# Hash attention followed by a SwiGLU block: VectorE's order at the ends of groups, and both rows of a pair in sequence

## The chip, the core and the metric

The kernel runs on one core of a Trainium2 chip. Its time is the device time of one execution in microseconds; the comparison uses the median of several runs. A core has a matrix engine (TensorE: PE in the profile, with the weight loads on a row of their own, PEld), a vector engine (VectorE: DVE), a scalar engine (ScalarE: ACT), a general engine (GpSimd: POOL) and a queue engine (SyncE: SP). Each works through its own list of instructions, and they wait for each other through semaphores.

## The reference

Two blocks follow each other. The first is attention in which a query sees only the keys with the same hash:

```python
# q, k, v: (4, 8, 768, 64), proj: (64, 6), all float32
q_bits = (np.einsum('bhsd,dk->bhsk', q, proj) > 0)      # six sign bits for each row
k_bits = (np.einsum('bhsd,dk->bhsk', k, proj) > 0)
mask = q_bucket[:, :, :, None] == k_bucket[:, :, None, :]
scores = np.where(mask, scale * np.matmul(q, k.transpose(0, 1, 3, 2)), -1e9)
attn = np.exp(scores - max); attn = attn / (attn.sum(-1) + 1e-09)
x = np.matmul(attn, v)                                   # then (B, H, S, D) -> (B*S, H*D) = (3072, 512)
```

The second is a gated feed-forward block on the 3072 rows that come out:

```python
g = x @ w_gate                       # 512 -> 1536
silu = g * (1.0 / (1.0 + np.exp(-g)))
out = (silu * (x @ w_val)) @ w_out   # 1536 -> 512
```

## The kernel before

There are four batches `b`, and in each of them four pairs of heads, so sixteen pairs `n`. A pair has two rows (`half`): 384 queries against all 768 keys, in six steps `c` of 128 keys. One row is a stage of TensorE: 36 matmuls for the scores (tile `sc`) and 24 for the product with `v` (tile `av`). ScalarE takes the exponentials, VectorE adds up the six tiles of them (`acc`). After both rows of a pair, `total` sums `acc` over the keys on TensorE (tile `sum`), takes the reciprocal on VectorE and spreads it by DMA; `norm` later multiplies it in. After a batch's last pair its feed-forward work is put on the list `atoms`.

```python
    def add(u):                     # after each step c of a row, on VectorE
        if c == 1:
            acc[n, half] = att.tile([P, 2, HQ], FP32, tag="acc", name="acc")
            nc.vector.scalar_tensor_tensor(out=acc[n, half], ...)              # L523
        elif c > 1:
            nc.vector.tensor_tensor(acc[n, half], acc[n, half], a[:, :, 0:HQ], op=ALU.add)  # L527
    def total(n):
        ps = ... bank("sum")
        for h in range(2):
            for half in range(2):
                nc.tensor.matmul(ps[g : g + BLOCK, 0:HQ], ones, t[half][:, h, :], ...)   # L540
        nc.vector.reciprocal(r, ps[:, 0:HQ])                                   # L548
        ...                                                  # eight DMAs spread r over t
        waiting.append(lambda: norm(n, t))                                     # L560, VectorE
        if pr == NP - 1:
            push_ffn(b)
```

The feed-forward work of a batch is nine groups: six up groups (both up projections and the gate) and three down groups (one chunk of 128 columns for each of the two rows). Both are written as Strassen products: fewer matmuls on TensorE, paid for with additions on VectorE. In batches 1 to 3 an up group has ten steps (68 matmul records in the profile). Two of its seven products are split once more (`deeper`), and the weights of these inner products are formed on VectorE by `weigh`, four additions of 128x128 (`r3`, `r2`, `r1`, `r4`). A function `look_ahead` calls `weigh(0)` of the group that stands first on `atoms`, if it has not been called yet.

```python
    def look_ahead():
        if atoms:
            finish(getattr(atoms[0][1], "ahead", []))

            def weigh(d):
                for o, p, q, op in ((r3, v11, v21, ALU.subtract), (r2, v22, r3, ALU.subtract),
                                    (r1, r2, v11, ALU.add), (r4, v12, r2, ALU.subtract)):
                    plus(o, p, q, op)
            ...
            def step(at):
                if at == 0:
                    while first:           # the batch's additions on x: 16 of them, once a batch
                        first.pop(0)()
                    finish(ahead)          # weigh(0), if it is not done yet
                for do in todo[at]:
                    do(at)
                if at == len(todo) - 1:
                    look_ahead()
                    settle(at + NB)        # what is left of the gates of this group
            # steps 0, 1: two outer products; step 2 begins with inner products on v11, r1, v12
```

The down part needs sums of the hidden values. `combine(i, 1)` forms `s1`, `combine(i, 2)` `s2`, `combine(i, 3)` `s3` in place, `combine(i, 4)` `s4`; each is done in two halves over the hidden blocks, `part` 0 and 1. Part 0 of the first chunk is `early`, which is tied to the last step of the last up group:

```python
    def down_strassen(out_of):
        def chunk(i):
            def step(n):
                if n == 0 and i == 0:
                    while next(preparing, None):
                        pass
                    for which in (1, 2, 3):
                        combine(0, which, 1)
                a, w, to = ((a11, b11, "a"), (s1, t1, "b"), (s2, t2, "a"), (a12, b21, "c"),
                            (s3, t3, "a"), (s4, b22, "b"), (a22, t4, "a"))[n]
                product(c, [(a[:, f], w[:, f]) for f in range(NFP)], ...)     # 12 matmul records
                ...
                for part in range(2):
                    if n == 0:
                        combine(i, 4, part)
                    elif n in (3, 4) and i + 1 < CH:
                        for which in ((1,), (2, 3))[n - 3]:
                            combine(i + 1, which, part)
        ...
        return lambda: [combine(0, which, 0) for which in (1, 2, 3)]

    def push_ffn(b):
        up_strassen(x, b, first)
        at = len(atoms) - 1
        early = down_strassen(out_of)
        size, last, end = atoms[at]
        atoms[at] = (size, lambda: (early(), last()), end)
```

The main loop goes over the 32 rows. From pair 4 on, every row is followed by a stretch of groups from `atoms` (a "gated stretch"). Groups are taken whole, as long as a credit is above zero: 14 units a row at first, and 15.75 from pair 8 (the third batch of pairs) on; a group is 14 units. In between stand the next pair's preparations (`chores`): two transposes on VectorE (`turn_q`, `turn_k`) and the hashes (TensorE tile `hps`, then ScalarE, a DMA and VectorE). What is left of `atoms` after the last row is done in one go, which is called the tail below.

```python
    for u in range(0, N, NCH):
        n, half, _ = units[u]
        gating = u >= LATE                                   # from pair 4 on
        ...
        for c in range(NCH):
            score(u + c)                                     # PE sc, ACT exp
            if c:
                add(u + c)
        if n >= 2 * NP:
            look_ahead()
        if ... or (n >= 2 * NP and half == 0):
            finish(waiting)                                  # norm of the pair before
        for c in range(NCH):
            attend(u + c)                                    # PE av
        if half == 1:
            load(n + 2, "qkv" if n + 2 > NP else "v")
        finish(first)                                        # the batch's 16 additions on x
        if half == 1 and n >= NP:
            total(n)
            if n + 1 < len(pairs):
                chores = [None] + steps.pop(0)()             # hashes: before the groups
        if not gating:
            continue
        if n + 1 < len(pairs) and half == 0:
            steps = front(n + 1)
            chores = [None, steps.pop(0), None, steps.pop(0)]   # both transposes
        credit += 14 if n < 2 * NP else 15.75
        while atoms and (credit > 0 or not end):
            size, atom, end = atoms.pop(0)
            credit -= size
            atom()
            ...                                              # chores, one for each unit
    for _, atom, _ in atoms:                                 # the tail
        atom()
```

Of the kernel before, what the change touches and what calls it, by code (L numbers as in the profile page):

```python
# [18 lines left out]
def kernel(  # L19
# [13 lines left out]
    B, H, S, D = q.shape  # L33
# [3 lines left out]
    CH = NCH // 2  # L37
    HQ = CH * P
    BLOCK = 32
    NP = H // 2  # L40
# [28 lines left out]
    def bank(name):  # L69
        return banks.tile([P, 512], FP32, tag="ps", name=name)  # L70


    pairs = [(b, pr) for b in range(B) for pr in range(NP)]
# [34 lines left out]
    def load(n, names):  # L108
        if n < len(pairs):
            for name in names:  # L110
                fetch(n, name, nc.sync)
# [83 lines left out]
    NB = 7  # L195
# [67 lines left out]
    def as_words(t):  # L263
        return t.bitcast(I32).rearrange("p (f w) -> p f w", w=2)

    spots = [hid[:, half, m].rearrange("p f q -> p (f q)") for half in range(2) for m in range(2)]
    early = [as_words(t[:, 0 : 2 * PIECE]) for t in spots]
# [33 lines left out]
    def scale_ahead():  # L301
        scale_to(min(progress["piece"] + 4, progress["scaled"] + 1))
# [70 lines left out]
    def prepare_on(n):  # L373
        for _ in range(n):
            next(preparing, None)
# [9 lines left out]
    atoms = []  # L385
# [195 lines left out]
    def finish(todo):  # L581
        while todo:
            todo.pop(0)()
# [6 lines that stand above are left out]
    def product(ps, pairs_, start):  # L590

        for i, (a, x) in enumerate(pairs_):
            nc.tensor.matmul(ps, a, x, start=start and i == 0, stop=i == len(pairs_) - 1,  # L593
                             skip_group_check=True)

    def plus(o, a, b, op=ALU.add):
        nc.vector.tensor_tensor(o, a, b, op=op)  # L597
# [162 lines left out]
        for i in range(NG // 2):  # L760
            both(i)

    def down_strassen(out_of):


        t2, t3, t4 = down_t
        t1 = b12
        s2, s1, s4 = down_s

        def parts(i, fs):  # L770
            return [hid[:, half, m, fs, i * P : (i + 1) * P]
                    for half in range(2) for m in range(2)]

        def combine(i, which, part):
            fs = slice(part * NFP // 2, (part + 1) * NFP // 2)
            a11, a12, a21, a22 = parts(i, fs)
            if which == 1:
                plus(s1[:, fs], a21, a22)
            elif which == 2:
                plus(s2[:, fs], s1[:, fs], a11, ALU.subtract)  # L780
            elif which == 3:
                plus(a21, a11, a21, ALU.subtract)
            else:
                plus(s4[:, fs], a12, s2[:, fs], ALU.subtract)

        def chunk(i):
            now = {}

            def step(n):
                a11, a12, s3, a22 = parts(i, slice(None))  # L790
                if n == 0 and i == 0:
                    while next(preparing, None):
# [4 lines that stand above are left out]
                    for name in "cba":  # L797
                        now[name] = bank("po")[:, 0:HD]
                    o = word_room[0]
                    now["o"] = [[o[:, (2 * r + x) * HD : (2 * r + x + 1) * HD] for x in range(2)]  # L800
                                for r in range(2)]
                a, w, to = ((a11, b11, "a"), (s1, t1, "b"), (s2, t2, "a"), (a12, b21, "c"),
                            (s3, t3, "a"), (s4, b22, "b"), (a22, t4, "a"))[n]
                c = now[to]
                product(c, [(a[:, f], w[:, f]) for f in range(NFP)], n in (0, 1, 3))
                r, x = ((0, 0), (1, 1), (0, 1), (0, 0), (1, 1), (0, 1), (1, 0))[n]
                o = now["o"][r][x]
                if n in (3, 4, 5):
                    plus(o, o, c)
                else:  # L810
                    nc.scalar.copy(o, c)  # L811
                if n >= 3:
                    nc.sync.dma_start(out_of(r, i)[:, x * HD : (x + 1) * HD], o)
                for part in range(2):
                    if n == 0:
                        combine(i, 4, part)
                    elif n in (3, 4) and i + 1 < CH:
                        for which in ((1,), (2, 3))[n - 3]:
                            combine(i + 1, which, part)

            for n in range(NB):
                atoms.append((2, lambda n=n: step(n), n == NB - 1))

        for i in range(CH):
            chunk(i)
        return lambda: [combine(0, which, 0) for which in (1, 2, 3)]

    def push_ffn(b):
        x = [xT[b, pr] for pr in range(NP)]
        rows = out[b * S : (b + 1) * S, :].rearrange("(p c) m -> p c m", c=NCH)  # L830

        def out_of(half, i):
            return rows[:, half * CH + i, :]

        up_strassen(x, b, first)
        at = len(atoms) - 1
        early = down_strassen(out_of)
        size, last, end = atoms[at]
        atoms[at] = (size, lambda: (early(), last()), end)

# [6 lines left out]
    def prepare_pair(count):  # L849
        for _ in range(count):  # L850
            rest.extend(f for f in steps.pop(0)() or [] if f)
# [4 lines left out]
    credit = 0.0  # L856
    for u in range(0, N, NCH):
        n, half, _ = units[u]
        gating = u >= LATE
        if u == MOVE:  # L860
            progress["late"] = True
            for t in late_ring:
                nc.gpsimd.memset(t[:, :, HQ:AW], 1.0)
        for c in range(NCH):
            score(u + c)
            if u + c == 2 or not gating and half == 1 and c == 2:
                prepare_pair(1)
            if c == 1 and half == 0 and 0 < n <= NP:
                total(n - 1)
            if c:  # L870
                add(u + c)
        if n >= 2 * NP:
            look_ahead()
        if (n < NP and half == 1) or u == LATE or (n >= 2 * NP and half == 0):
            finish(waiting)
        finish(rest)
        if not gating and half == 0:
            steps = front(n + 1)
        if not gating and half == 0 and u > 0:
            prepare_pair(2)  # L880
        for _ in range(1 if u else 2):
            scale_ahead()
        for c in range(NCH):
            attend(u + c)
        if not gating:
            scale_ahead()
        if half == 1:
            load(n + 2, "qkv" if n + 2 > NP else "v")
        elif not gating:
            prepare_pair(2 if u > 0 else 4)  # L890
            if n + 2 <= NP:
                load(n + 2, "qk")
        finish(first)
        prepare_on(0 if u == LATE else 4)
        chores = []
        if half == 1 and n >= NP:
            total(n)
            if n + 1 < len(pairs):
                chores = [None] + steps.pop(0)()
        prepare_on(0 if LATE - NCH <= u <= LATE else 3 if gating or not half else 1)  # L900
        if not gating:
            continue
        if n + 1 < len(pairs) and half == 0:
            steps = front(n + 1)
            chores = [None, steps.pop(0), None, steps.pop(0)]

        credit += 14 if n < 2 * NP else 15.75
        end = True
        part = 0
        while atoms and (credit > 0 or not end):  # L910
# [3 lines that stand above are left out]
            part += size  # L914
            if n < 2 * NP and part >= 11 or u + NCH == N and part >= 6:
                finish(waiting)
                if u + NCH == N:
                    finish([first.pop(0) for _ in range(min(2, len(first)))])
            if 5 < part < 14 if u == LATE else part < (9 if u < LATE + 3 * NCH else 11):
                prepare_on(size)  # L920
            if 6 < part < 11 or u == LATE and part > 10:
                scale_ahead()
            for _ in range(size):
                if chores:
                    step = chores.pop(0)
                    chores.extend(step and step() or [])
        while chores:
            step = chores.pop(0)
            chores.extend(step and step() or [])
    for _, atom, _ in atoms:  # L930
        atom()


# [30 lines left out]
```

The softmax here doesn't subtract the row's maximum and nothing guards it: scores larger than these inputs give would overflow.

## Time and profile before

| what | value |
|---|---|
| time, median of 3 runs | 995.05 us (994.68 to 995.08) |
| span of the profiled execution | 992.9 us |
| PE busy | 980.0 us, 99% |
| DVE busy | 670.4 us, 68% |
| ACT busy | 408.1 us, 41% |
| POOL busy | 127.3 us, 13% |
| granted clock of TensorE | 0.999 |
| HBM traffic over the span | 100 GB/s |

In the profile a busy share says how long an engine had an instruction of its own under way. Ends of matmuls are modelled, so for TensorE it is safer to read where the next matmul starts. The chain of waits follows the work that ended last back through the program: a piece on PE means that TensorE was the one everybody waited for then, a piece on DVE or ACT in the middle of PE pieces means that TensorE stood still until that instruction was done. All additions through the helper `plus` carry line L597, all Strassen matmuls L593; they are told apart by tile: `up` and `po` are the PSUM tiles of the up and down groups, `inner` holds the formed inner weights of `weigh(0)`, `room` (128x384) the down sums `s1`, `s2` and `s4`.

### The profile page before, as it was taken

To read this page: it belongs to the slowest core of one execution; us is meant where nothing else is said; L and a number is where in the kernel's file an instruction comes from. 1 tells how busy PE (TensorE), PEld (TensorE's weight loads), DVE (VectorE), ACT (ScalarE), POOL (GpSimd) and SP (SyncE) were. 2 spreads that over 40 slices of the span, in tenths; PEclk is the share of its full clock that TensorE was granted. 3 is DMA by queue.
4 is the path that set the end of the run, shared out by engine and by line. 5 is a ranking of instruction groups with operands and counts; after the bars stand their busy time and mean duration, and the time that the engine had idled before them with its cause. 6 is when DMAs were issued, how large, how long until landed. Compare 5 with 4: busy or idle time off the path is not lost.

```text
span 992.9 us, 13575 instructions
## 1 busy us (share of the span) xinstructions
PE 980.0 (99%) x4813; PEld 625.0 (63%) x4813; DVE 670.4 (68%) x1276; ACT 408.1 (41%) x921; POOL 127.3 (13%) x248
## 2 busy tenths in 40 slices
PE   9999999999999999999999999999999999999998
PEld 4444555555577766656566775666666786666687
DVE  5899888888965556777784457776776446667631
ACT  7999555566512234444442313443342202323200
POOL 3222232231100011111010001111100001121000
PEclk9999999999999999999999999999999999999999
DMA  8777685875303042433322114343121112233001
GB/s 235 218 249 229 157 259 178 228 269 157 106 26 76 16 121 79 104 92 84 99 81 57 52 31 108 98 107 100 57 87 33 35 34 85 75 117 105 1 30 35
DMA packets 119987, 107.02 MB, mean 108 GB/s; under 512 B 90032, under 2 KB 104848, under 8 KB 119920
## 3 DMA queue, kind: packets, MB, share of 16 engines
q0 software_dynamic: 18336, 73.29, 23.0%
q1 hardware_dynamic: 100784, 32.67, 14.2%
q8 instruction: 38, 0.62, 0.3%
q10 hardware_dynamic: 800, 0.20, 0.1%
q14 instruction: 29, 0.24, 0.1%
HBM read 81.79 MB, written 17.30 MB: 100 GB/s over the span
## 4 chain that ended last, share of the span: by engine, by line
PE 91%; DVE 5%; issue 2%; ACT 2%; POOL 0%; DMA 0%; DVEq 0%; ACTq 0%; POOLq 0%
PE up L593 41%; PE po L593 21%; PE sc L494 14%; PE av L509 11%; PE sum L540 1%; PE hps L412 1%; DVE c L571 1%; DVE hid L575 1%; PE tps L396 1%; DVE hid L597 1%; DVE room L368 0%; DVE inner L597 0%; PE idle L134 0%; DVE acc L527 0%; ACT th L570 0%
## 5 line engine op out<-in xcount | busy, mean ns | idle before, releaser
L593 PE MATMUL up<-xT,room 128*128 128x384 f32 (+1 forms) x732 | 243.0, 465 | 0.0
L593 PEld LDWEIGHTS up<-xT,room 128*128 128x128 f32 x732 | 134.8, 190 | 73.3 <-issue 9.8
L593 PE MATMUL up<-xc,room 128*128 128x384 f32 (+1 forms) x540 | 176.9, 455 | 0.0
L327 POOL DMA_DIRECT2D room<-ram x144 | 77.9, 543 | 677.8 <-PE up L593 662.4
L494 PE MATMUL sc<-qT,kT 64*128 64x384 f32 x768 | 161.0, 494 | 0.0
L597 DVE TENSOR_TENSOR c<-c,up 128x192 f32<-128x192 f32 (+1 forms) x198 | 78.9, 406 | 80.9 <-PE up L593 76.5
L527 DVE TENSOR_TENSOR acc<-acc,A 128x768 f32<-128x768 f32 x128 | 122.7, 958 | 15.7 <-ACT A L497 2.9
L593 PEld LDWEIGHTS up<-xc,room 128*128 128x128 f32 x540 | 99.2, 190 | 43.8 <-DVE c L597 1.1
L570 ACT ACTIVATE th<-c 128x384 f32<-128x384 f32 x90 | 46.9, 522 | 158.1 <-DVE c L571 89.7
L497 ACT ACTIVATE A<-sc 128x384 f32<-128x384 f32 x256 | 103.9, 528 | 0.6 <-PE sc L494 0.5
L494 PEld LDWEIGHTS sc<-qT,kT 64*128 64x128 f32 x768 | 67.9, 186 | 54.3 <-issue 40.5
L811 ACT COPY words<-po 128x256 f32<-128x256 f32 x48 | 17.9, 373 | 199.0 <-PE po L593 180.1
L597 DVE TENSOR_TENSOR hid<-hid,up 128x192 f32<-128x192 f32 (+1 forms) x162 | 67.5, 418 | 43.5 <-PE up L593 41.6
L509 PE MATMUL av<-A,vraw 128*64 128x384 f32 (+1 forms) x512 | 88.2, 486 | 0.0
L597 DVE TENSOR_TENSOR words<-words,po 128x256 f32<-128x256 f32 x36 | 15.2, 421 | 99.2 <-PE po L593 99.2
L679 ACT COPY c<-up 128x384 f32<-128x384 f32 x72 | 34.4, 478 | 88.8 <-PE up L593 88.7
L593 PE MATMUL po<-wo,room 128*128 128x256 f32 x288 | 66.6, 380 | 1.5 <-DVE room L597 1.5
L593 PE MATMUL po<-wo,hid 128*128 128x256 f32 x288 | 66.9, 382 | 0.0
L593 PE MATMUL po<-room,hid 128*128 128x256 f32 x288 | 66.1, 379 | 0.0
L509 PEld LDWEIGHTS av<-A,vraw 128*64 128x64 f32 x512 | 36.7, 137 | 46.1 <-issue 44.1
L494 PE MATMUL sc<-qb,kb 64*128 64x384 bf16 x384 | 65.1, 323 | 0.5 <-DVE kb L426 0.5
L593 PEld LDWEIGHTS po<-wo,hid 128*128 128x128 f32 x288 | 54.1, 190 | 12.1 <-issue 4.9
(137 smaller groups left out, 1165.3 us busy)
## 6 DMA issues: line engine op xcount, KB each, us to landing
room<-ram POOLq DMA_DIRECT2D x96, 384.0 KB, 3.7
vraw<-in_v_dram SPq DMA_DIRECT2D x16, 384.0 KB, 3.3
ram<-room POOLq DMA_DIRECT2D x12, 512.0 KB, 5.1
room<-ram POOLq DMA_DIRECT2D x48, 128.0 KB, 3.5
out_dram<-words SPq DMA_DIRECT2D x48, 128.0 KB, 1.7
room<-in_moe_w_out_dram POOLq DMA_DIRECT2D x10, 512.0 KB, 6.4
qraw<-in_q_dram SPq DMA_DIRECT2D x48, 96.0 KB, 3.2
hid<-in_moe_w_gate_dram POOLq DMA_DIRECT2D x9, 512.0 KB, 6.8
```

Of the source, the lines that this page charges most:

```text
L327: nc.gpsimd.dma_start(places[k % 2][:, PARTS[go], :], ram[k % NG][:, PARTS[go], :])
L396: nc.tensor.transpose(ps[:, i * P : (i + 1) * P], raws[name, n][:, half * CH + i, :, :].rearrange("p h d -> p (h d)"), ident)
L412: nc.tensor.matmul(tile_[i * BLOCK : (i + 1) * BLOCK, 0:HQ], hash_w, T[name, n][:, half * HQ : (half + 1) * HQ], start=True, stop=True)
L494: nc.tensor.matmul(sc[h], x["k", n][rows, ks], x["q", n][rows, qs], start=start, stop=not start)
L497: nc.scalar.activation(weights(u)[:, h, 0:HQ], sc[h], AF.Exp, scale=SCALE * (OFF / 2 if n <= NP else 1.0))
L509: nc.tensor.matmul(ps[h * D : (h + 1) * D, 0:width], raws["v", n][:, h, c, :], a[:, h, 0:width], start=c == 0, stop=c == NCH - 1)
L527: nc.vector.tensor_tensor(acc[n, half], acc[n, half], a[:, :, 0:HQ], op=ALU.add)
L570: nc.scalar.activation(th, g, AF.Tanh, scale=0.5)
L593: nc.tensor.matmul(ps, a, x, start=start and i == 0, stop=i == len(pairs_) - 1, skip_group_check=True)
L597: nc.vector.tensor_tensor(o, a, b, op=op)
L679: nc.scalar.copy(tile_of(g, spot), c)
L811: nc.scalar.copy(o, c)
```

## The change

Three places put VectorE's instructions at the end of a group in another order, and one changes the large order of work.

1. The tail now takes each group off the list before it runs it, so that `look_ahead` at the end of a group finds the next group there instead of the first one of the tail.
2. In the last batch the first down chunk takes its fourth product (on `a12`) as the second one, so that `s1` is needed one product later.
3. In all batches but the last, `early` comes after the last step of the last up group rather than before it.
4. From pair 8 on (`whole`), both rows of a pair follow each other, and one gated stretch with the credit of both (31.5) follows. The next pair's transposes and loads come in its first group, the hashes after its first 14 units; the norm of the pair before and the batch's additions on x stay behind the first row.

```diff
-    def down_strassen(out_of):
+    def down_strassen(out_of, at_once):
...
-            def step(n):
+            order = (0, 3, 1, 2, 4, 5, 6) if at_once and i == 0 else range(NB)
+
+            def step(at):
+                n = order[at]
...
-                    elif n in (3, 4) and i + 1 < CH:
-                        for which in ((1,), (2, 3))[n - 3]:
+                    elif at in (3, 4) and i + 1 < CH:
+                        for which in ((1,), (2, 3))[at - 3]:
...
-        early = down_strassen(out_of)
+        early = down_strassen(out_of, b == B - 1)
         size, last, end = atoms[at]
-        atoms[at] = (size, lambda: (early(), last()), end)
+        atoms[at] = (size, lambda: (early(), last()) if b == B - 1 else (last(), early()), end)
...
+        whole = n >= 2 * NP
...
-        if n >= 2 * NP:
+        if whole and half:
             look_ahead()
...
-        if half == 1:
+        if whole:
+            pass
+        elif half == 1:
             load(n + 2, "qkv" if n + 2 > NP else "v")
...
-            if n + 1 < len(pairs):
+            if n + 1 < len(pairs) and not whole:
                 chores = [None] + steps.pop(0)()
...
-        if not gating:
+        if not gating or whole and not half:
             continue
-        if n + 1 < len(pairs) and half == 0:
+        if n + 1 < len(pairs) and whole:
+            turn_q, turn_k, hashes = front(n + 1)
+            chores = 5 * [None] + [turn_q, None, turn_k, lambda: load(n + 2, "qkv")]
+            chores += 5 * [None] + [hashes]
+        elif n + 1 < len(pairs) and half == 0:
             steps = front(n + 1)
             chores = [None, steps.pop(0), None, steps.pop(0)]
-        credit += 14 if n < 2 * NP else 15.75
+        credit += 31.5 if whole else 14
...
-    for _, atom, _ in atoms:
-        atom()
+    while atoms:
+        atoms.pop(0)[1]()
```

## The prediction

> **What bounds the kernel now.** I read the page first (busy shares, granted clock), then the waits of TensorE alone, then the chain of waits in order of time, and last the timelines of PE and DVE at the joints which these point to.
>
> ```profile
> PE 980.0 (99%) x4813; PEld 625.0 (63%) x4813; DVE 670.4 (68%) x1276; ACT 408.1 (41%) x921; POOL 127.3 (13%) x248
> PEclk9999999999999999999999999999999999999999
> ```
>
> TensorE has matmuls under way for 99% of the span, at full clock. A change that removes no matmul can therefore win only where TensorE stands still, or where matmuls follow each other more slowly than their kind needs. The waits of TensorE (total us, times, longest):
>
> ```profile
> PE up L593 <- DVE inner L597: 5.7, 5, 1.1
> PE po L593 <- DVE room L597: 1.5, 2, 1.0
> ```
>
> Five waits for the inner weights and two for the down sums: 7.2 us that this view admits. The chain of waits (start, length, what) shows where. In the tail:
>
> ```profile
> 822.10 17.50 PE up L593 x68
> ...
> 839.62 0.56 DVE hid L597
> 840.17 0.48 DVE c L571
> ...
> 840.68 0.53 ACT th L570
> ...
> 841.23 0.56 DVE c L571
> ...
> 842.18 0.55 DVE hid L575
> 842.73 0.21 DVE inner L597
> ...
> 843.29 0.30 DVE inner L597
> ...
> 843.63 14.86 PE up L593 x58
> ...
> 862.53 14.86 PE up L593 x58
> ```
>
> A group that nothing disturbs takes 17.50 us (68 records). In the tail, groups begin their inner products 862.53 - 843.63 = 18.90 us apart. The loss is 1.40 us a joint, and its cause stands between: `weigh` (inner) comes after the whole chain of gates of the group before. The same chain earlier, at the row after a batch's last up group, and at the first row of the third batch of pairs:
>
> ```profile
> 323.74 5.05 PE sc L494 x36
> 328.79 4.04 PE av L509 x24
> 332.83 18.33 PE po L593 x84
> ...
> 507.17 3.47 PE sc L494 x21
> 510.68 2.30 PE sc L494 x13
> 512.99 4.04 PE av L509 x24
> ```
>
> Scores take 5.05 us elsewhere, but 512.99 - 507.17 = 5.82 us here (and 5.81 us at 747.61): 0.77 us lost each time. The timeline of DVE there has the three `early` additions from 506.50 to 508.03, in front of the group's last additions. Those free the PSUM banks which the scores need. The two `po` waits are 654 + 104 ns late at 280.4 (start to start, against the usual 216 ns) and 1155 + 104 ns late at 938.95.
>
> **What the Trainium skill says.** "TensorE: Matmul & The Clock Gate", section Architectural detail, calls VectorE and ScalarE strict FIFOs, while TensorE may only pull weight loads ahead. The trace agrees: `inner` at 842.73 does nothing that needs the gates, and still waits behind a gate which waits for a ScalarE instruction (840.68 to 841.21). So the order in the program decides. "Perfetto Trace Analysis", section Optimization Strategy, advises to find the gaps on the busiest engine and what blocks them, and to make those dependencies start sooner; that is what changes 1 to 3 do. "TensorEngine Tiling (Array Packing)", section Key Properties, states that changing the tiling mode drains TensorE; that would be the reason for change 4. The trace shows a price: the last `up` record before a row's scores is followed 93 ns later than usual, and the second score record another 201 ns later; from `av` to `up` it is 100 and then 104 ns.
>
> **The change part by part.**
>
> *1. Tail.* Six up groups, five joints. After it `weigh` stands behind the group's last plus and two gate instructions, before the gate that waits for ScalarE. That order already runs in the gated stretches of the kernel before: there the group's last plus starts at 452.11 and `r1` ends at 454.45, 2.34 us later. At the tail's joint the last plus starts at 839.62, so `r1` would be ready at 841.96. TensorE's first product on `inner` would follow the record of 842.16 by 163 ns, at 842.32. There are 0.36 us to spare, the wait goes wholly: 5 x 1.40 = 7.0 us.
>
> *2. First down chunk of the last batch.* `s1` part 1 is ready at 938.90. With `a12` second, the product on `s1` begins two products of 12 x 0.216 = 2.59 us after 933.91, at 939.09, and its second half later still. `a12`'s last block is written by the gates that end at 938.3, and its last two records start at 933.91 + 22 x 0.216 = 938.66: that fits. Gain 1.155 + 0.104 = 1.26 us.
>
> *3. `early` behind the last step.* At 507 and 748 the banks come free 1.5 us earlier, the scores run through: 2 x 0.77 = 1.5 us. In batch 0 only the order changes. The 0.76 us at 280.4 comes from a VectorE that is full from 257 to 281, and stays.
>
> *4. Rows in sequence.* For each of eight pairs one exit `av` to `up` (204 ns) and one entry `up` to `sc` (294 ns) become one `av` to `sc`, which costs 101 + 201 = 302 ns in the first pairs (75.14 us): 0.196 x 8 = 1.6 us. Against it, the hashes of seven pairs now stand between groups instead of beside the sum. Sum and hashes together took 1.59 us from the first `sum` record to the first `up` record (377.63 to 379.22), the sum alone 0.77 us (784.80 to 785.57), so the hashes cost 0.82 us there. Between two `up` records I take 0.78 + 0.09 + 0.10 = 0.97 us, and up to 0.33 us more than before where the sum is the short kind: 7 x 0.15 to 0.33, about -1.3 us. What is left of part 4 itself: +0.3 us.
>
> The new cost lies in VectorE behind the first row. In the third and the fourth batch of pairs, at its first pair (8 and 12), 16 additions on x stand between the two rows. In the kernel before a gated stretch followed them, now the second row's `acc` additions do, and `sum` waits for those:
>
> ```profile
> 327.62 4.14 DVE L527 TENSOR_TENSOR acc<-acc,A 128x768 f32<-128x768 f32 x4
> 331.68 1.02 DVE L597 TENSOR_TENSOR xc<-xT 128x384 f32<-128x384 f32 x2
> ...
> 338.05 0.36 DVE L597 TENSOR_TENSOR words<-xc,words 128x192 f32<-128x192 f32 x1
> ```
>
> Pair 8: the row starts on TensorE at 323.74. The first row's sums are done at 331.68 (+7.94 us), the additions at 338.32 (+6.64), and five more `acc` instructions take 5.13 us (326.55 to 331.68): 343.45, that is 19.71 us after the start. TensorE has both rows done after 2 x 9.09 = 18.2 us, and waits 1.5 us. Pair 12: the norm of 0.93 us comes in too (572.12 to 573.05), so 20.65 us and a wait of 2.5 us. Sum: -4.0 us. At the other pairs the second row's sums are done 7.9 us after its start, within its 9.1 us.
>
> In all: 7.0 + 1.3 + 1.5 + 0.3 - 4.0 = 6.1 us. 995.05 - 6.1 = 988.95, said as 989.0 us.
>
> **The rivals.**
> *A. All joints are clean, and the additions on x hide.* Then 4.0 us more, 985.0 us. For it: VectorE is busy only 68%. Against it: the sum cannot start before the last `acc`, and VectorE keeps its order.
> *B. The wait moves into the new joints.* From pair 8 on, six joints between up groups lie inside a stretch; if each loses the 1.40 us of the tail, 8.4 us go and the time is 997.4 us. For it: at these joints no row of 9.1 us lies between any more, and the first group carries the reciprocal of 2.56 us and two transposes of 0.9 us. Against it: `look_ahead` works there as in the gated stretches before (454.45), and VectorE is busy 12.46 of 18.90 us in a tail group, with gaps of 1.13 and 0.86 us where the transposes fall.
> *C. The loads collide.* The loads of q, k and v are now issued when the next group's weights are fetched (POOL's `room<-ram`, landing 3.6 us after issue). If they doubled that to 7 us, the weights fetched about 8.5 us before the next group would still be there in time. Little, some 1 to 2 us at worst.
> *D. Change 4 saves far more, because the switch is dearer than it looks.* Against it: nothing but the 0.2 us a pair shows in the starts of matmuls.
>
> **Range and chances.** All of the sure gains together (7.0 + 1.3 + 1.5 + 1.6 us) make 11.4 us or 1.1%, so 2% faster (975.1 us) is out of reach. 2% slower (1014.9 us) would need 26 us of new waits, more than rival B and the sums' waits together. Within the range the sums' waits (3 to 5 us) and the new joints (0 to 3 us) decide; 985.5 to 992.5 us should hold it. Faster by over 2%: 0.01, within: 0.97, slower: 0.02.
>
> **What would show it.** In the changed profile the waits of TensorE for `inner` should be gone, and the chain should show six tail groups 17.5 us apart, without DVE pieces. Scores of 5.05 us should stand where 5.82 us was. Two waits of `sum` for `acc` (L540 for L527), of 1.5 and 2.5 us, should be new, at the first pair of the third and fourth batch of pairs. A wait of `po` for `room` should remain once, near 280 us. I am wrong if `inner` still holds up `up` inside the stretches (B), if no wait for `acc` appears (A), or if the scores of the second row wait.

## The result and the profile after

| | before | after |
|---|---|---|
| time, median | 995.07 us (994.68 to 995.16, 4 runs) | 989.68 us (989.58 to 989.87, 4 runs) |
| span of the profiled execution | 992.9 us | 988.0 us |
| PE busy | 980.0 us | 978.8 us |
| DVE busy | 670.4 us | 669.3 us |

The ratio is 0.9947 with a 95% interval of 0.9930 to 0.9964: 5.4 us or 0.5% faster, where 6.1 us and 989.0 us were predicted. The engines do the same work as before; what changed is how long TensorE stands still. The waits of TensorE in the changed kernel (total us, times, longest):

```profile
PE sum L540 <- DVE acc L527: 2.7, 2, 1.8
...
PE po L593 <- DVE room L597: 0.5, 1, 0.5
PE po L593 <- ACT words L815: 0.5, 1, 0.5
```

The five waits for `inner` are gone and one of the two for `room` as well. Two waits of `sum` for `acc` are new, as predicted, and so is one of `po` for `words`, which was not. The chain of waits of the changed kernel (start, length, what) shows the tail and the last down groups:

```profile
770.26 54.59 PE po L593 x252
824.84 104.89 PE up L593 x408
929.73 10.37 PE po L593 x48
940.11 0.02 issue
940.13 0.38 ACT words L815
940.51 0.04 issue
940.55 44.31 PE po L593 x204
```

Six up groups run as one piece of 104.89 us, which is 17.48 us a group; before, a group and its joint took 18.90 us. From the first `up` record of the tail to the first `po` record it is 104.89 us now and was 111.98 us (821.94 to 933.91), so 7.1 us are won. But four products into the last batch's first down chunk TensorE waits for a ScalarE copy. The sum of pair 8, in the chain of the same kernel:

```profile
326.66 0.97 DVE acc L523
...
331.88 0.94 DVE xc L597 x2
...
338.16 0.36 DVE words L597
338.52 0.88 DVE acc L523
...
342.68 0.97 DVE acc L527
343.65 0.04 issue
343.69 0.85 PE sum L540 x6
344.54 18.33 PE po L593 x84
```

For 17 us this chain runs over VectorE: `acc` of the first row, the additions on x, `acc` of the second row, then the sum. A long piece of VectorE in the chain does not mean that TensorE stands still all that time: it works on both rows meanwhile, starts the sum's first record at 341.93 and only then has to wait. From the first `sum` record to the next `po` record it is 2.54 us here and 3.40 us at pair 12, against 0.78 us at the other pairs: 1.76 + 2.62 = 4.4 us. (The view of waits says 2.7 us, as it counts from the modelled end of two `sum` records that could start early.)

An undisturbed pair of the changed kernel in the same chain:

```profile
398.81 5.05 PE sc L494 x36
...
416.96 0.78 PE sum L540 x8
417.75 18.97 PE up L593 x72
436.72 0.78 PE hps L412 x8
437.50 16.39 PE up L593 x64
453.89 1.32 PE sc L494 x7
```

From scores to scores it takes 453.89 - 398.81 = 55.08 us. The same pair took 55.10 us before (from 396.97 to 452.07). The rows in sequence bring 0.02 us at such a pair.

### The profile page after: what moved, and what is told of

It reads as the page before. It is cut to its first block, busy times and chain, and to the rows that moved or that the text cites. A ratio compares the mean times of both kernels' runs of the same rounds, so it can differ in the third digit from the quotient of the medians.

```text
span 988.0 us, 13667 instructions
## 1 busy us (share of the span) xinstructions
PE 978.8 (99%) x4813; PEld 621.7 (63%) x4813; DVE 669.3 (68%) x1276; ACT 409.7 (41%) x921; POOL 127.2 (13%) x248
## 4 chain that ended last, share of the span: by engine, by line
PE 90%; DVE 6%; ACT 2%; issue 2%; POOL 0%; DMA 0%; DVEq 0%; ACTq 0%; POOLq 0%
PE up L593 42%; PE po L593 22%; PE sc L494 13%; PE av L509 10%; DVE acc L527 2%; PE sum L540 1%; PE hps L412 1%; ACT A L497 1%; DVE xc L597 1%; PE tps L396 1%; DVE room L368 0%; ACT room L497 0%; PE idle L134 0%; DMA room<-ram 0%; DVE acc L523 0%
```

## The experiments

Times are medians. Each was compared with the kernel before on the same chip, which stood at 994.95 to 995.19 us every time. Spans are those of the profiled execution.

### The tail's list alone (change 1 in the kernel before)

```diff
-    for _, atom, _ in atoms:
-        atom()
+    while atoms:
+        atoms.pop(0)[1]()
```

> The kernel before with the tail's list handling alone (change 1). Theory: the five waits for the inner weights go, 5 x 1.40 = 7.0 us, so 988.1 us; the tail's up groups take 105 us instead of 112 us on TensorE, nothing else moves. Rival: the gates that now come later hold up something else in the next group (PSUM banks, the gate tiles), and only part of the 7 us comes; then 990 to 994 us, and a new wait of up appears.

988.26 us (988.07 to 988.91), ratio 0.9931 (0.9917 to 0.9946). No wait for `inner` is left, the waits for `room` are both there as before:

```profile
PE po L593 <- DVE room L597: 1.5, 2, 1.0
```

So two lines bring 6.8 us, more than the whole change does.

### Both rows in sequence alone (changes 1 to 3 undone)

```diff
-            order = (0, 3, 1, 2, 4, 5, 6) if at_once and i == 0 else range(NB)
+            order = range(NB)
...
-        atoms[at] = (size, lambda: (early(), last()) if b == B - 1 else (last(), early()), end)
+        atoms[at] = (size, lambda: (early(), last()), end)
...
-    while atoms:
-        atoms.pop(0)[1]()
+    for _, atom, _ in atoms:
+        atom()
```

> The changed kernel with changes 1 to 3 undone, so both rows in sequence alone. Theory: the two waits of the sum for the last acc cost 1.8 + 2.6 = 4.4 us, and the switches saved around the rows come back around the hashes, so 995.1 + 4.3 = 999.4 us; joints inside the stretches are clean. Rival (switches saved, hashes free): 8 x 0.2 us less, 997.8 us. Rival (joints inside a stretch cost 1.4 us): about 1004 us or more.

999.01 us (998.79 to 999.25), ratio 1.0039 (1.0025 to 1.0053): slower than before by 3.9 us. The waits of TensorE are all of the old ones and the new one:

```profile
PE up L593 <- DVE inner L597: 5.7, 5, 1.1
PE sum L540 <- DVE acc L527: 2.7, 2, 1.8
PE po L593 <- DVE room L597: 1.5, 2, 1.0
```

The five waits for `inner` are those of the tail; none was added at the joints inside the stretches. This rules out the prediction's rival B for this kernel.

### Changes 1 to 3 without the sequence

The kernel before with these parts of the change; the main loop stays as it was.

```diff
+            order = (0, 3, 1, 2, 4, 5, 6) if at_once and i == 0 else range(NB)
...
-        atoms[at] = (size, lambda: (early(), last()), end)
+        atoms[at] = (size, lambda: (early(), last()) if b == B - 1 else (last(), early()), end)
...
-    for _, atom, _ in atoms:
-        atom()
+    while atoms:
+        atoms.pop(0)[1]()
```

> Changes 1 to 3 without the rows in sequence. Theory: 7.1 (tail) + 1.55 (scores after early) + 0.5 (last down chunk, where one wait is replaced by a shorter one) = 9.2 us less than before, 985.9 us, that is faster than the changed kernel by 3.8 us. Rival: the sequence of rows is needed for those gains or brings some itself; then not under 988 us.

985.78 us (985.72 to 985.88), ratio 0.9905 (0.9891 to 0.9920): 9.3 us faster than before and 3.9 us faster than the whole change. Its chain, where the scores took 5.82 us in two pieces before:

```profile
507.13 5.05 PE sc L494 x36
512.18 4.04 PE av L509 x24
```

### The additions on x behind the second row

```diff
-        finish(first)
+        if not whole or half:
+            finish(first)
```

> The changed kernel with the batch's 16 additions on x put behind the second row (after its acc additions) instead of behind the first. Theory: both waits of the sum go, 4.4 us, 985.3 us. Rival: the additions only move the wait: the reciprocal and the down sums come 6.6 us later, and the next down group or up group waits for VectorE; then 987 to 990 us, with a new wait of po or up for room, xc or inner.

985.81 us (985.27 to 985.88), ratio 0.9904 (0.9890 to 0.9919), 3.9 us faster than the change. The wait of `sum` is gone, and no other came in its place. In the chain pair 8 now runs on TensorE alone:

```profile
333.34 5.04 PE sc L494 x36
338.39 4.02 PE av L509 x24
342.41 0.78 PE sum L540 x8
343.19 18.33 PE po L593 x84
```

The reciprocal of that pair starts at 347.93, 5.5 us after its sum began, and no wait of TensorE comes of it. By the starts of matmuls, the stretch from the first row of pair 8 to the first `up` record of the tail is 496.54 us long instead of 500.90: 4.36 us less, the two waits whole. In the profiled execution the row itself starts 0.41 us later (324.19 instead of 323.78), although nothing in front of it was changed, so the difference of the times is smaller.

### Another order of the last batch's first down chunk

```diff
-            order = (0, 3, 1, 2, 4, 5, 6) if at_once and i == 0 else range(NB)
+            order = (0, 3, 2, 1, 4, 5, 6) if at_once and i == 0 else range(NB)
```

This stands on top of the run before this one.

> As the run with the additions behind the second row, and the last batch's first down chunk in the order 0, 3, 2, 1, 4, 5, 6 instead of 0, 3, 1, 2, 4, 5, 6, so that another product stands between the two on the PSUM bank a. Theory (product 4 adds to the bank that product 2 has just filled and must wait for ScalarE's copy of it): the wait of 0.6 + 0.1 us goes, 0.7 us less, 984.6 us, and no wait of po is left in the last 60 us. Rival (ScalarE's copy is late for its own reasons, or s2 is not ready in time): the wait stays or becomes a wait for room, 985.3 us.

984.92 us (984.74 to 985.15), 0.9 us less by the medians, 0.6 us by the spans, and 0.72 us from the first to the last record of the last down groups (54.90 and 54.18 us by their starts). Products 0, 2, 4 and 6 add up in PSUM bank `a`, and between them ScalarE or VectorE reads it. With product 4 right behind product 2, TensorE had to wait until ScalarE had copied the bank (the copy at 940.13 in the chain above). In the new order product 1, on bank `b`, lies between them. The timeline of PE in this run shows no idle time:

```profile
930.86 2.75 PE L593 MATMUL po<-room 128*128 128x256 f32 x12
933.45 2.75 PE L593 MATMUL po<-wo,room 128*128 128x256 f32 x12
936.04 2.75 PE L593 MATMUL po<-room,hid 128*128 128x256 f32 x12
```

### The same order without the sequence of rows

```diff
-            order = (0, 3, 1, 2, 4, 5, 6) if at_once and i == 0 else range(NB)
+            order = (0, 3, 2, 1, 4, 5, 6) if at_once and i == 0 else range(NB)
```

This stands on top of changes 1 to 3 alone.

> Changes 1 to 3 without the rows in sequence, with that other order of the last batch's first down chunk. Theory (the sequence of rows is worth nothing in itself): 985.9 - 0.7 = 985.2 us, within 0.7 us of the sequence with the waits mended. Rival (each pair in sequence saves 0.2 us of switching): the sequence is ahead by 1.6 us.

985.19 us (984.84 to 985.59), span 982.9 us, against 984.92 us and 983.4 us with the sequence. The two cannot be told apart. A net saving of 1.6 us by the sequence is ruled out as long as the hashes stand between the groups.

### The inner weights behind all gates

```diff
-                    look_ahead()
                     settle(at + NB)
+                    look_ahead()
```

> The changed kernel with the next group's inner weights formed after the last gates of a group, everywhere. Theory: the tail's five joints lose 1.40 us each again (7.0), the two joints inside stretches without hashes lose 1.40 (2.8), the four where the hashes give TensorE 0.98 us of other work lose 0.42 (1.7): 11.5 us more, 1001.2 us. Rival (inside the stretches other work covers it): only the tail, 996.7 us.

1001.53 us (1001.31 to 1003.46), ratio 1.0065 (1.0048 to 1.0082), 11.9 us slower than the change. The wait of TensorE for `inner` is now there at all eleven joints, not just at the five of the tail:

```profile
PE up L593 <- DVE inner L597: 8.7, 11, 1.2
```

By the starts of matmuls, the stretch behind pair 8 has 35.30 us of `up` after its hashes instead of 33.87 us (1.43 us for one joint), and the one behind pair 9 has 16.82 instead of 16.39 us (0.43 us, as the hashes cover the rest). So the joints inside the stretches are clean in the change because `look_ahead` puts four small additions ahead of the last gates.

### `early` in front of the last step again

```diff
-        atoms[at] = (size, lambda: (early(), last()) if b == B - 1 else (last(), early()), end)
+        atoms[at] = (size, lambda: (early(), last()), end)
```

> The changed kernel with change 3 undone: early before the last step in all batches. Theory: the first row after the up groups of batches 1 and 2 has its scores at 5.82 instead of 5.05 us again, 2 x 0.77 = 1.5 us more, 991.2 us. Rival (the sequence of rows takes that wait up, as the second row's scores follow at once): no difference, 989.7 us.

991.41 us (991.12 to 992.87), 1.7 us slower than the change. The scores break in two again, in its chain:

```profile
509.05 3.47 PE sc L494 x21
512.52 0.04 issue
512.56 2.31 PE sc L494 x13
514.86 4.04 PE av L509 x24
```

### The other order in all batches

```diff
-            order = (0, 3, 2, 1, 4, 5, 6) if at_once and i == 0 else range(NB)
+            order = (0, 3, 2, 1, 4, 5, 6) if i == 0 else range(NB)
```

> The kernel with the additions behind the second row and the other order of the last batch's first down chunk, with that order (0, 3, 2, 1, 4, 5, 6) in the first down chunk of all four batches. Theory: batch 0's wait of po for room near 280 us (0.65 + 0.1 us) goes too, as s1 is needed two products later, 984.9 - 0.75 = 984.2 us; in batches 1 and 2 nothing changes. Rival: VectorE is full there until 281 us, and s2 part 1 is what now comes late; the wait stays, perhaps shorter, 984.5 to 984.9 us.

983.98 us (983.74 to 984.35), with the sequence. The last wait of `po` for `room` is gone: the first down group of batch 0 takes 18.33 us by the starts of its matmuls instead of 19.08 us.

### The hashes beside the sum

```diff
+            if n == 2 * NP - 1:
+                turn_q, turn_k, hashes = front(n + 2)
+                chores += 2 * [None] + [turn_q, turn_k, lambda: load(n + 3, "qk")]
+            if n + 1 < len(pairs) and whole:
+                *signs, spread_q, spread_k = hashes()
...
-            turn_q, turn_k, hashes = front(n + 1)
-            chores = 5 * [None] + [turn_q, None, turn_k, lambda: load(n + 2, "qkv")]
-            chores += 5 * [None] + [hashes]
+            turn_q = turn_k = None
+            if n + 2 < len(pairs):
+                turn_q, turn_k, hashes = front(n + 2)
+            chores = [None] + signs + [turn_q, spread_q, turn_k]
+            chores += [lambda: (load(n + 3, "qk"), load(n + 2, "v")) and None]
+            chores += 6 * [None] + [spread_k]
```

This stands on top of the run before. `hashes()` issues the matmuls and returns the steps behind them: `signs` on ScalarE, `spread_q` with a DMA, and `spread_k` with two instructions of VectorE on `kb`.

> The same, with the next pair's hashes back beside the sum, ahead of the groups (its transposes and loads come one pair earlier for that). Theory: the entry and the exit that the hashes cost TensorE between the groups, 0.09 + 0.10 us, go at seven pairs; a pair of batches 1 to 3 then takes 54.9 instead of 55.08 us, 1.3 us in all, 982.9 us. Rival (what counts is only the waits): no difference, 984.2 us. Against both: transposes or loads that come too early collide with something, a new wait.

983.91 us (983.80 to 984.04): nothing won. The time is as the rival said, but the cause is not: pairs 8, 11 and 12 became faster by 0.33 us each, and the four whose stretch is two up groups got a new wait.

```profile
PE up L593 <- DVE c L597: 1.3, 4, 0.3
```

Its timeline of DVE shows what stands in the way:

```profile
436.30 1.02 DVE L575 SCALAR_TENSOR_TENSOR hid<-c,hid 128x384 f32<-128x384 f32 x2
437.33 0.85 DVE L426 TENSOR_SCALAR kb<-kb,columns 32x768 bf16<-32x768 bf16 x2
438.11 0.33 DVE L597 TENSOR_TENSOR c<-c,up 128x192 f32<-128x192 f32 x1
```

The `kb` instructions, the last step of the hashes, come straight behind the gates of the first group. The addition after them empties the PSUM bank that the next inner product wants to add to, and so that product starts late:

```profile
438.50 0.59 PE L593 MATMUL up<-inner 128*128 128x192 f32 x2 [0.33 <-DVE c L597]
```

By the starts of matmuls it is 0.50 us late, and the next record another 0.10 us.

### Changes 1 to 3 with the other order in all batches

```diff
-            order = (0, 3, 2, 1, 4, 5, 6) if at_once and i == 0 else range(NB)
+            order = (0, 3, 2, 1, 4, 5, 6) if i == 0 else range(NB)
```

This stands on top of the other order without the sequence of rows.

> Changes 1 to 3 without the rows in sequence, with the order 0, 3, 2, 1, 4, 5, 6 in the first down chunk of all batches. Theory: 985.2 - 0.75 = 984.4 us, within 0.5 us of the sequence with the same mends and over 1 us above the one with the hashes beside the sum.

984.58 us (984.06 to 985.09), 10.5 us faster than before without any change of the large order. It is 0.6 us above the two runs before it, which is within the spread of its own runs. By the starts of matmuls, the stretch from the first row of pair 8 to the first `up` record of the tail is 496.72 us here and 496.52 us with the sequence and the hashes between the groups, so no more than 0.20 us of it comes from the sequence there. That the hashes beside the sum would be over 1 us ahead was wrong, for the new wait just shown.

### The hashes beside the sum, their last step later

```diff
-            chores += 6 * [None] + [spread_k]
+            chores += 11 * [None] + [spread_k]
```

> The kernel with the hashes beside the sum, and VectorE's last step of the hashes (two instructions of 0.4 us on kb) five units later, where the kernels without that move have it. Theory: those two instructions, right behind the gates of the first group, were what product 2 of the next group waited for at four pairs (0.5 + 0.1 us each); without them a pair takes 54.74 instead of 55.08 us (0.33 us, seen at the pairs without that wait), 7 x 0.33 = 2.3 us less than with the hashes between the groups, 981.7 us, and no wait of up is left. Rival (the wait belongs to the new place of the hashes as such): 983.9 us, and up still waits for VectorE's c.

981.65 us (981.38 to 981.83), ratio 0.9864 (0.9848 to 0.9881): the fastest of all, 13.5 us faster than before. No wait of `up` is left, and the pair shown above has in its chain:

```profile
395.99 5.04 PE sc L494 x36
401.03 4.04 PE av L509 x24
405.07 5.05 PE sc L494 x36
410.12 4.02 PE av L509 x24
414.14 0.78 PE sum L540 x8
414.92 0.65 PE hps L412 x8
415.57 35.16 PE up L593 x136
450.73 5.04 PE sc L494 x36
```

From scores to scores it is 54.74 us, against 55.08 us in the change. Only with the hashes out of the way is the sequence of rows worth something.

How much of that is the sequence itself can be read against the kernel with changes 1 to 3 and the other order in all batches. From the first row of pair 8 to the tail it takes 496.72 us by the starts, the fastest kernel 494.18 us: 2.54 us. Eight pairs save 0.20 us each on switches of TensorE (35.16 instead of two times 17.68 us of `up`), 1.6 us in all. The other 0.96 us is something else: at six pairs, `sum` and `hps` together take 1.43 instead of 1.59 us, as told in the last section.

## Why the prediction was right, point by point

**Tail.** Predicted 7.0 us, measured 7.1 us on TensorE and 6.8 us for the two lines alone. Estimating `r1` from the order that already ran in the gated stretches held. At the tail's first joint in the changed kernel `r1` ends 2.34 us after the group's last plus again (842.36 to 844.70), and TensorE's first product on `inner` starts at 845.07. The 0.37 us to spare are what was predicted (0.36 us).

**First down chunk of the last batch.** Predicted 1.26 us, measured 0.53 us (55.44 to 54.90 us from the first to the last record of the last down groups). This is the step that failed. The wait for `s1` went as computed, but a wait of 0.62 + 0.10 us for ScalarE's copy took its place, as product 4 now adds to the bank that product 2 has just filled. The prediction checked that the operands of the moved product were ready, not what the moved product had separated before. The run with products 1 and 2 exchanged removed that wait.

**`early` behind the last step.** Predicted 1.5 us, measured 1.55 us by the lengths of the scores. Undoing it cost 1.7 us. Batch 0's wait stayed, as said. That it had to stay because VectorE is full there was not so: with `s1` needed two products later, in the other order in all batches, it went.

**Rows in sequence.** Predicted +0.3 us for switches and hashes together, measured 0.2 us: from the first row of pair 8 to the tail the change takes 500.90 us by the starts and the kernel before 498.27 us, and the sum's waits (4.4 us) less the scores' gain (1.5 us) explain all but 0.2 us of that. A pair with up groups gains 0.02 us. The saving around the rows is real, but the hashes between groups need an entry and an exit of their own: 18.97 + 16.39 = 35.36 us of `up` are exactly the two times 17.68 us of before. With the hashes beside the sum the same records take 35.16 us, so the switches saved are 0.20 us a pair, as predicted, and `sum` and `hps` are 0.13 us shorter besides: the 0.33 us a pair of that run. One reading was wrong, in a way that cancels. The second score record comes 104 ns late (427 instead of 323 ns after the first), not 201 ns; the other 97 ns lie at the end of the scores, where `av` follows after 259 instead of 162 ns. They stood in the entry from `up` and in the one from `av` alike.

**The additions on x.** Predicted 1.5 and 2.5 us, measured 1.76 and 2.62 us by the starts, and 3.9 us of time when they were moved (4.36 us by the starts).

The terms add up to 7.1 + 0.5 + 1.55 + 0.2 - 4.4 = 5.0 us; the spans differ by 4.9 us and the medians by 5.4 us. Of the rivals, A was wrong (the additions did not hide), B did not happen and is shown to depend on `look_ahead`, and no collision of loads (C) appeared. D was wrong: a pair saves 0.20 us of switches, no more, and the hashes use that up in the change as it stands. The 2.3 us won at last (983.98 to 981.65 us) needed two more moves, and not all of it is switches.

## What to carry to other kernels

Where one engine is busy 99% of the time, list the places where its starts are late, and look for the instruction of another engine that stands in front of the one it needs: moving four small additions ahead of a gate was worth more here than a new order of whole stages. When work is moved, check three things: what it needs, what it now stands in front of (the additions on x), and what it used to keep apart (two products on one PSUM bank). A large change of order that wins nothing may be paying for it elsewhere: test its parts alone, since three of the four parts here were better without the fourth as it stood.

## What was not expected of the hardware

Beside the sum, the hashes cost TensorE 0.33 us a pair less than between the groups, where 0.19 us of entry and exit were expected. By the starts of matmuls, `sum` and `hps` take 0.67 + 0.76 us side by side (in the fastest kernel from 414.07 and 414.74, with `up` at 415.50), but 0.78 + 0.78 us apart (in the change 416.89 to 417.68 and 436.65 to 437.43). So `sum` is 0.11 us shorter where `hps` follows it, whose records are 128x32 like its own, than where `up` with its 128x128 follows.

The kernel before has them side by side as well, and still takes 0.67 + 0.92 = 1.59 us at six pairs (8 to 10 and 12 to 14), against 0.67 + 0.76 = 1.43 us at pairs 7 and 11. At pair 8 the first of the four `sum` records that run side by side starts 0.17 us before the other three, and the `hps` records behind them are staggered in the same way; with the rows in sequence all four start within 0.02 us. What staggers them was not tried.
